# Statistics, first loads and first matmuls of a linear-attention and MLP kernel: eps as a third group, both first tiles on one queue, duplicates on GpSimd

## The chip, the cores and the metric

One core of a Trainium2 chip. The metric is the device time of one execution in microseconds (us); single executions of one kernel differ by 1 to 2 us here, so medians and ratios over several runs are given. A run is called slow when it is over 1.5% above the fastest of its kernel in the same rounds; ratios use the others, the fast runs, alone. Each profile is one execution, with its own span (a little shorter than the device time).

## The reference, cut to what matters

```python
x = A_x                                  # 1 x 2048 x 448, bf16
xn = _layernorm(x, axis=-1)              # (x - m) / sqrt(v + 1e-5)
return x + _A_ref(xn, A_wqkv, A_w_phi, A_wo) + _B_ref(xn, B_w1, B_w2)
# A: linear attention with softmax feature maps, 16 heads of 28
# B: silu(xn @ w1) @ w2, w1 is 448 x 1792
```

Everything needs xn. The kernel has sixteen tiles of 128 rows. The first tiles are normalised on VectorE, transposed on TensorE and go at once into xn @ w1 ("F1"); the later ones are prepared behind that work.

## The kernel before

The loads are issued from two queues, SP's and ScalarE's. w1 comes as three blocks of 448 KB and two small pieces:

```python
load_x(0, 1)                 # tile 0, 112 KB, SP queue
load_x(1, 2, eng="act")      # tile 1, ScalarE queue
load_w1(0, "sp")             # weight block 0 ("first")
load_w1(1, "act")            # block 1 ("second")
load_x(2, 3, eng="act")
load_w1(2, "sp")             # block 2 ("third")
# ... two last pieces of w1, tile 3; w_phi in 56-byte rows; then wqkv, wv, w2
```

The statistics of a tile, with eps added by an instruction of its own, and the power on GpSimd:

```python
bn_stats(st6[:, t, :], x_sb[:, t, :])                        # VectorE
bn_aggr(mv[:, t, :], st6[:, t, :])                           # VectorE: mean, variance
tensor_scalar(ve[:, t], mv[:, t, 1:2], EPS_LN, None, add)    # VectorE (tiles 0-3) or GpSimd
tensor_tensor(rstd[:, t], ve[:, t], neghalf, pow)            # GpSimd
tensor_scalar(xnd[:, t, a:b], x[a:b], mean, rstd, subtract, mult)   # VectorE, in parts
```

TensorE's order at the start; every TensorE instruction keeps this place:

```python
warm(10)                     # 10 pairs of 512-column matmuls on a constant
X_tr(0) ... f1a(0, 0, 0)     # transposes of tile 0; 4 pairs on block 0
X_tr(1, first part)
f1a(0, 1, 0, 1)              # pairs that alternate between block 0 and block 1
...                          # block 1, then block 2, then the last pieces of w1
X_tr(2), F1B, X_tr(3), FT_tr(0), c0(0, 0), ...
```

A "pair" is two matmuls on the two halves of the array's rows (64 rows each; the second starts at most 0.04 us after the first). So the second weight block is needed at the second pair of `f1a(0, 1, 0, 1)`.

The softmax here doesn't subtract the row's maximum and nothing guards it: scores larger than these inputs give would overflow.

## Time and profile before

| | before |
|---|---|
| device time, median of the runs beside the changed kernel | 149.38 us (148.97 to 150.09, 4 runs) |
| span of the profiled run | 147.4 us |
| TensorE busy | 142.0 us, 96% of the span |
| first matmul on w1 | 6.41 us |
| second weight block: issued, landed | 1.34 us, about 6.25 us |
| start of the long stretch without waits | 20.00 us |

How to read it: the kernel ends 127.4 us after that last moment. (The prediction starts from 149.68 us, the median of three runs.) The head ends when TensorE is through its first 20 us of work, so a change in the head shows as a shift of that one number.

### The profile page before, as it was taken

The numbers are of one execution on the slowest core, as the hardware profiler recorded it, in microseconds if no ns is written. First come the engines' busy times: TensorE is split into PE (matmuls) and PEld (weight loads), VectorE is DVE, ScalarE is ACT, GpSimd is POOL, SyncE is SP. The second block draws the span as 40 slices with busy tenths as digits, with TensorE's granted clock in tenths as the row PEclk, the third lists the DMA queues.
The fourth block names the chain that finished last, engine by engine and source line by source line (L and its number), as shares of the span: only waits on it lengthen the run. The fifth ranks groups of instructions, "written<-read, shape, count | busy, mean of one in ns | idle before, by whom it ended". The sixth has DMA issues, their size and how long they took to land.

```text
span 147.4 us, 4912 instructions
## 1 busy us (share of the span) xinstructions
PE 142.0 (96%) x2118; PEld 86.7 (59%) x2118; DVE 96.4 (65%) x182; ACT 85.3 (58%) x109; POOL 84.5 (57%) x95
## 2 busy tenths in 40 slices
PE   6999999999999999999999999999999999999990
PEld 2589965555556555555555556655566666666550
DVE  1877379999995596941077997870154874948533
ACT  4248789898758785976986758598571111011110
POOL 3326026059999959899023999999972204022220
PEclk9999999999999999999999999999999999999998
DMA  4996989965929893389730091333769234843323
GB/s 127 388 266 150 296 257 275 118 139 170 146 55 112 174 167 86 90 188 134 174 67 0 0 111 36 71 76 73 73 145 101 52 105 125 129 132 76 103 71 125
DMA packets 43710, 19.10 MB, mean 130 GB/s; under 512 B 36713, under 2 KB 43049, under 8 KB 43689
## 3 DMA queue, kind: packets, MB, share of 16 engines
q1 hardware_dynamic: 43032, 17.87, 61.6%
q10 hardware_dynamic: 656, 0.92, 1.9%
q8 instruction: 16, 0.26, 0.8%
q14 instruction: 6, 0.04, 0.1%
HBM read 8.17 MB, written 1.84 MB: 68 GB/s over the span
## 4 chain that ended last, share of the span: by engine, by line
PE 96%; DVE 0%; POOL 0%; DVEq 0%; issue 0%; ACT 0%; POOLq 0%
PE psum L448 95%; PE psum L461 1%; DVE x_sb L827 0%; DVEq L1124 0%; POOL hT L487 0%; ACT xT L466 0%; POOL neghalf L486 0%; DVEq L1113 0%; POOLq L1158 0%
## 5 line engine op out<-in xcount | busy, mean ns | idle before, releaser
L715 POOL TENSOR_TENSOR E<-E,Rk 128x896 bf16<-128x896 bf16 x32 | 53.3, 1697 | 7.1 <-DVE Rk L710 5.1
L448 PE MATMUL psum<-xT,w_sb 64*128 64x512 bf16 (+2 forms) x522 | 46.7, 323 | 0.3 <-ACT xT L466 0.2
L448 PE MATMUL psum<-w_sb,hT 64*128 64x448 bf16 x448 | 45.2, 349 | 0.0
L448 PEld LDWEIGHTS psum<-w_sb,hT 64*128 64x128 bf16 x448 | 24.1, 94 | 16.6
L708 DVE TENSOR_REDUCE Sk<-E 128x64 f32<-128x1792 bf16 x16 | 31.9, 2004 | 2.9 <-ACT E L466 2.9
L466 ACT ACTIVATE hT<-psum 128x1024 bf16<-128x1024 f32 (+1 forms) x29 | 28.0, 992 | 9.5 <-PE psum L448 9.1
L448 PEld LDWEIGHTS psum<-xT,w_sb 64*128 64x128 bf16 x522 | 25.0, 94 | 13.9 <-issue 0.3
L466 ACT ACTIVATE E<-psum 128x896 bf16<-128x896 f32 x32 | 27.4, 917 | 6.4 <-PE psum L448 5.3
L466 ACT ACTIVATE xT<-psum 128x448 f32<-128x448 f32 (+3 forms) x14 | 6.6, 475 | 32.0 <-PE psum L448 27.8
L448 PE MATMUL psum<-wqk,xT 64*128 64x448 bf16 x224 | 23.6, 349 | 0.0
L779 POOL TENSOR_TENSOR xT<-xT,x_sb 128x448 f32<-128x448 f32 x8 | 8.3, 1033 | 25.0 <-ACT xT L466 21.5
L448 PEld LDWEIGHTS psum<-wqk,xT 64*128 64x128 bf16 x224 | 12.2, 94 | 8.6
L583 POOL TENSOR_TENSOR rstd<-ve,neghalf 128x1 f32<-128x1 f32 x16 | 9.1, 569 | 7.5 <-DVE ve L581 6.8
L767 POOL TENSOR_TENSOR Ye<-Ye,x_sb 128x448 f32<-128x448 f32 x8 | 8.1, 1034 | 8.9 <-DVE Ye L765 8.9
L591 DVE TENSOR_SCALAR xnd<-x_sb,mv,rstd 128x896 bf16<-128x896 bf16 x12 | 8.3, 723 | 5.8 <-POOL rstd L583 5.7
L575 DVE BATCH_NORM_STATS2 st<-x_sb 128x6 f32<-128x448 bf16 x16 | 9.6, 604 | 3.7 <-DMA x_sb<-in_A_x_dram 3.7
L448 PE MATMUL psum<-wv_sb,xT 64*128 64x448 bf16 x112 | 12.0, 349 | 0.0
L765 DVE TENSOR_TENSOR Ye<-psum,Ye 128x448 f32<-128x448 f32 x8 | 5.0, 621 | 10.3 <-ACT Ye L466 10.2
L448 PE MATMUL psum<-wo_sb,E 64*128 64x448 bf16 x112 | 11.3, 349 | 0.0
L804 DVE TENSOR_TENSOR E<-psum,rden 128x224 bf16<-128x224 f32 x32 | 10.3, 384 | 0.4
L448 PEld LDWEIGHTS psum<-wo_sb,E 64*128 64x128 bf16 x112 | 6.2, 94 | 4.4
L448 PEld LDWEIGHTS psum<-wv_sb,xT 64*128 64x128 bf16 x112 | 5.9, 94 | 4.0
(47 smaller groups left out, 102.9 us busy)
## 6 DMA issues: line engine op xcount, KB each, us to landing
w_sb<-in_B_w_dram SPq DMA_DIRECT2D x4, 448.0 KB, 5.4
out_dram<-x_sb SPq DMA_DIRECT2D x8, 224.0 KB, 2.2
w_sb<-in_B_w_dram SPq DMA_DIRECT2D x4, 336.0 KB, 5.2
x_sb<-in_A_x_dram SPq DMA_DIRECT2D x2, 448.0 KB, 5.0
wv_sb<-in_A_wqkv_dram SPq DMA_DIRECT2D x2, 392.0 KB, 5.4
wo_sb<-in_A_wo_dram SPq DMA_DIRECT2D x14, 56.0 KB, 2.3
phT<-in_A_wqkv_dram SPq DMA_DIRECT2D x3, 224.0 KB, 4.0
w_sb<-in_B_w_dram ACTq DMA_DIRECT2D x1, 448.0 KB, 4.9
```

What stands on the lines that cost most here:

```text
L448: ins = e.matmul(dst, lhsT, rhs, start=st, stop=sp, skip_group_check=True)
L461: ins = e.transpose(dst, src, idn)
L466: return P.op("act", d_act(n), lambda e: e.activation(dst, src, func, scale=scale), reads=reads or [src], writes=writes or [dst], table=ta ...
L575: P.op("dve", 630, lambda e: e.bn_stats(st6[:, t, :], xs), [xs], [st6[:, t, :]], name="bnst", ordered=od)
L583: P.op("pool", 580, lambda e: e.tensor_tensor(rstd[:, t:t + 1], ve[:, t:t + 1], neghalf[:], ALU.pow), [ve[:, t:t + 1], neghalf[:]], [rstd[ ...
L591: dve(lambda e: e.tensor_scalar(dst, src, mv[:, t, 0:1], rstd[:, t:t + 1], ALU.subtract, ALU.mult), 734, [src, mv[:, t, 0:1], rstd[:, t:t ...
L708: dve(lambda e: e.tensor_reduce(Sk[:, t % 3, :].rearrange("p (h g) -> p h g", g=2), Er, AXL.X, ALU.add), d_dve(1792), [Er], [Sk[:, t % 3, ...
L715: pool(lambda e, Eh=Eh, Rb=Rb: e.tensor_tensor(Eh, Eh, Rb, ALU.mult), 1770, [Eh, Rh], [Eh], "phi%d" % qk)
L765: dve(lambda e: e.tensor_tensor(y, b, y, ALU.add), d_dve(D), [b, y], [y], "ye_d")
L767: pool(lambda e: e.tensor_tensor(y, y, x_sb[:, t, :], ALU.add), 1110, [y, x_sb[:, t, :]], [y], "ye_x")
L779: pool(lambda e: e.tensor_tensor(y, y, x_sb[:, t, :], ALU.add), 1110, [y, x_sb[:, t, :]], [y], "yl_x")
L804: dve(lambda e, dst=dst, src=src, rb=rb: e.tensor_tensor(dst, src, rb, ALU.mult), d_dve(224), [src, r], [dst], "o")
```

## The change

Its intent: bring xn of the first two tiles sooner and start the real work sooner. eps goes into the aggregation as a constant third group of statistics (count 0, mean 0, summed squares D*eps). Tiles 0 and 1 stand at the head of one queue, and the second weight block waits for a memset on GpSimd, so that it does not get ahead of them. Tile 0's and 1's 64-column duplicates go to GpSimd, the constant of the warm-up is written by VectorE, one warm-up pair goes, and F1 is put in another order to need the late loads later.

```diff
-        st6 = sb("st6", [128, NT, 6], F32)
+        st6 = sb("st6", [128, NT, 9], F32)
-        P.op("pool", 230, ... memset(wsrc, 1.0) ...)
+        P.op("dve", 230, ... memset(wsrc, 1.0) ...)
+        P.op("dve", 90, ... memset(st6[:, :, 6:9], 0.0) ...)
+        P.op("dve", 90, ... memset(st6[:, :, 8:9], D * EPS_LN) ...)
-        warm(10, d=427.0)
+        warm(9, d=427.0)
         load_x(0, 1)
-        load_x(1, 2, eng="act")
+        load_x(1, 2)
         load_w1(0, "sp")
-        load_w1(1, "act")
+        bd0 = P.op("pool", 300, ... memset(BD[:], 0.0) ...)
+        load_w1(1, "act", bd0)
+        load_w1(2, "sp")
         load_x(2, 3, eng="act")
-        load_w1(2, "sp")
# cut: tensor_scalar to ve goes; pow reads mv[:, t, 1:2]
# cut: xn's columns 448:512 of tiles 0 and 1 on "pool", ahead of the next tile's power
# cut: in F1, the last-64 pieces after the third block; F1B's second half ahead of X_tr(2)
-        c0(0, 0)
+        pads_init()                       # moved here, behind TensorE's mark
+        hold[0] = take()
+        for t in (2, 3):                  # 128-column pieces in place of 256
+            for u in range(2):
+                F1ph(0, hold[0], u * 256 + (t - 2) * 128, u, t * 128, 128, ...)
```

## The prediction

> **What bounds the kernel now.** I read the page's busy shares first, then the chain of waits, then the opening 13 us instruction by instruction, because everything in the diff lies there or in small statistics work off the path.

> ```profile
> PE 142.0 (96%) x2118; PEld 86.7 (59%) x2118; DVE 96.4 (65%) x182; ACT 85.3 (58%) x109; POOL 84.5 (57%) x95
> ...
> PE 96%; DVE 0%; POOL 0%; DVEq 0%; issue 0%; ACT 0%; POOLq 0%
> ```

> The first line is busy time by engine, the second the chain that ended last, by engine. TensorE is both the busiest engine and nearly the whole chain. In order of time the chain has these pieces (start us, length us, what):

> ```profile
> 0.88 0.47 POOL hT L487
> 1.35 0.05 issue
> 1.39 4.45 PE psum L448 x14
> 5.84 0.13 PE psum L461 x4
> 5.97 0.02 issue
> 5.99 0.28 ACT xT L466
> 6.28 0.14 issue
> 6.41 0.44 PE psum L448 x8
> ...
> 20.00 123.70 PE psum L448 x1725
> ```

> Three things are to be seen. From 20.00 to 143.70 there is only matmul. I summed the matmul pairs of that stretch from the program [...]: about 123 us. So this stretch runs at the array's rate, and nothing in it can be won by a helper engine. Second, the stretch from 6.41 to 20 has almost no waiting either; by the same sum it holds about 12.7 us of work in the 14.4 us from 5.63 on, and most of the missing time lies before 7.4. Third, the head: 4.45 us of warm-up matmuls on a constant, then transposes of x, an eviction, the first real matmul at 6.41. The change can only win by pulling 6.41 forward without opening holes behind it.

> What sets 6.41? The timeline of VectorE and GpSimd for the first tile:

> ```profile
> 3.19 0.63 DVE L575 BATCH_NORM_STATS2 st<-x_sb 128x6 f32<-128x448 bf16 x1 [3.19 <-DMA x_sb<-in_A_x_dram]
> 3.86 0.18 DVE L579 BATCH_NORM_AGGREGATE mv<-st 128x2 f32<-128x6 f32 x1
> 4.07 0.15 DVE L581 TENSOR_SCALAR ve<-mv 128x1 f32<-128x1 f32 x1
> 4.32 0.55 POOL L583 TENSOR_TENSOR rstd<-ve,neghalf 128x1 f32<-128x1 f32 x1 [2.25 <-DVE ve L581]
> ...
> 5.08 0.79 DVE L598 TENSOR_SCALAR xnd<-x_sb,mv,rstd 128x256 bf16<-128x256 bf16 x3
> 5.25 0.59 POOL L583 TENSOR_TENSOR rstd<-ve,neghalf 128x1 f32<-128x1 f32 x1 [0.38 <-DVE ve L581]
> 5.54 0.49 PEld L461 LDWEIGHTS psum<-ident,xnd 64*128 64x128 bf16 x10 [0.60 <-POOL rstd L583]
> ```

> x0 lands at 3.19; statistics, aggregation, the add of eps (ve), the power on GpSimd, then the first 256 columns of xn at 5.08, ready near 5.4, so its weight load is at 5.54. The warm-up queue ends at the same time: ten pairs 0.425 us apart from 1.39 make 5.64. Two limits are tied: shortening one alone wins nothing, and the change shortens both.

> [...] The ten transposes from 5.55 on average 241 ns, those after 6.35 only 190, so the clock opened near 6.2, almost 5 us after the first warm-up matmul. [...] from 4.2 us on the sum stands at some 430 GB/s, and a 448 KB weight block takes 4.0 us on SP's queue, 4.9 on ScalarE's.

> **The change part by part.**
> *eps in the aggregation.* A constant third group of statistics puts D*eps into the summed squares, so the aggregation gives var + eps. It removes ve: aggregation starts at 3.86, power at 4.32, a distance of 0.46. Without ve it is 0.18 + about 0.10 of semaphore = 0.28: power 4.14 to 4.69. VectorE also drops two ve instructions (each about 0.08 to 0.2 in its queue): second statistics near 4.0, second aggregation 4.65 to 4.83, first xn near 4.85 in place of 5.08. Gain 0.2 to 0.25. [...] For the other twelve tiles a 0.22 us GpSimd add goes (2.7 us of GpSimd in all), off the path: worth 0.
> *64-column duplicates of tiles 0 and 1 on GpSimd.* These take two instructions of about 0.30 us out of VectorE between xn0 and the evictions. On GpSimd I estimate 0.31 us: 0.22 for a one-column tensor_scalar (ve in later tiles) plus 63 x 1.48 ns, the slope between its 448- and 896-column products (1034 and 1697 ns). The first stands ahead of the second power: rstd1 runs about 5.0 to 5.6, against 5.25 to 5.84 before. So xn1 comes near 5.7 in place of 6.13: gain 0.4 for tile 1, just enough to keep up with tile 0.
> *Nine warm-up pairs.* Their start stays near 1.39 (VectorE's fill ends where GpSimd's did), their end moves from 5.64 to 1.39 + 9 x 0.425 = 5.2. Then xn is the limit: transposes near 5.3 in place of 5.63, the first real matmul near 6.05 in place of 6.41. Gain 0.35.
> *x0 and x1 on SP, second weight block behind a memset on ScalarE's queue.* x1 is issued 0.3 us later but alone behind x0, and its statistics are not due before 4.0; before it landed at 0.92 + 2.6 = 3.5. w1 block 0 landed at 1.24 + 4.0 = 5.2, over 1 us early. Block 1 landed at 6.25 (1.34 + 4.9); issued near 2.05 now, but less behind x1, I put it at 6.3 to 6.6. TensorE will ask for it at 6.3 to 6.4 (second pair of phase 1), so this may take 0 to 0.2 back. Block 2, x2 and x3 should land earlier than their 7.9, 8.1 and 9.36.
> *Order of the F1 groups, pads later.* Same number of matmul columns. Two 256-column pairs become 128-column pairs at 55 ns each against 109, so no array time is added. The third block's last-64 pieces come later, which removes the small slack of 0.35 us between their landing (8.8) and their use. The hole of about 0.05 us at 13.18 goes. The 2.5 us of pad memsets leave GpSimd's path of LN3: worth 0 to 0.1.
> *Sum.* +0.35 (start) + 0.05 (hole) + 0.05 (tile 1) - 0.1 (block 1) = 0.35. The clock takes some back: real work that starts earlier, with the warm-up starting at the same time, spends more of itself at half rate. [...] Net 0.25 to 0.3: 149.68 - 0.3 = 149.4.

> **The rivals.** (1) *The weight block takes over*: block 1, issued 0.7 us later, lands near 6.9 and TensorE waits for it at 6.3. For: it is last on the slower queue. Against: the engines carry x1 and block 0 sooner, so it shares less. It would make 149.7 to 149.9, no gain. (2) *LN3 becomes the wait*: X transposes of tiles 2 and 3 now stand back to back near 11.4 to 11.7, and before, xn3 was ready only near 12.07. For: x3 landed at 9.36 and three serial steps follow. Against: ve goes (0.2), the pads go, x3 should come 0.3 to 0.6 sooner. If it waits: 0.3 lost, 149.7. (3) *More is won than I count*: the stretch from 5.63 to 7.4 holds some 0.9 us of waiting; if the better order of VectorE closes half of it, gain 0.8, 148.9. [...]

> **Range and chances.** The change reaches at most the first 13 us of 149.68, of which about 1.7 us are not matmul work. Two per cent is 3.0 us, beyond all of it, so faster by over 2% is nearly excluded; slower by that needs a new hole of 3 us in a stretch that has none, in a program whose order on TensorE is fixed. Predicted 149.4 us. The spread of single executions (1.1 us before) exceeds the effect, so the range is 148.6 to 150.0. Chances: 0.01 faster, 0.98 within 2%, 0.01 slower.

> **What would show the steps right or wrong.** Right: no ve lines; the first power near 4.1; first xn near 4.85; transposes of x0 near 5.3; first matmul on w1 near 6.05; the chain's 123.7 us piece of the same length, beginning 0.3 us or so earlier; span near 147.1. Wrong: TensorE or its weight load idle behind a w1 landing near 6.4; a wait on xn near 11.5; the ones ending much after 1.4 on VectorE; matmuls of the first F1 group 289 ns long in place of 220 (a cold clock); the long piece longer than 124 us.

## The result, and the profile after

The changed kernel takes 153.88 us (152.52 to 154.34, 4 runs) against 149.38: slower, ratio 1.0281, 95% interval 1.0202 to 1.0359. Ratios here and below are the mean time of one kernel's fast runs over that of the other's of the same rounds, so not quite the ratio of the medians quoted beside them. The predicted 149.4, with 148.6 to 150.0 as its range, is missed.

The page of the changed kernel, busy time and the chain by engine:

```profile
PE 144.2 (95%) x2132; PEld 92.3 (61%) x2132; DVE 95.5 (63%) x179; ACT 85.4 (56%) x109; POOL 82.6 (54%) x84
...
PE 91%; DMA 5%; DVE 1%; issue 0%; POOL 0%; DVEq 0%
```

A transfer has come onto the chain. In order of time (start us, length us, what):

```profile
1.54 0.29 POOL ident L487
1.83 0.23 POOL BD L522
2.07 0.03 POOL phT L531
2.10 7.27 DMA w_sb<-in_B_w_dram
...
9.42 0.93 PE psum L447 x11
10.34 0.16 PE psum L460 x6
10.50 6.29 PE psum L447 x87
...
25.19 123.71 PE psum L447 x1716
```

The long stretch has its old length, 123.7 us, but begins at 25.19 in place of 20.00. The chain leads back through the second weight block, issued at 2.10 behind the memset of BD and landed 7.27 us later, at 9.37. The same load in the two kernels, its issues by queue (KB each, us to landing), first before, then after:

```profile
w_sb<-in_B_w_dram ACTq DMA_DIRECT2D x1, 448.0 KB, 4.9
```

```profile
w_sb<-in_B_w_dram ACTq DMA_DIRECT2D x1, 448.0 KB, 7.3
```

The start itself went as meant. VectorE's and GpSimd's timeline of the changed kernel:

```profile
2.91 0.63 DVE L577 BATCH_NORM_STATS2 st<-x_sb 128x6 f32<-128x448 bf16 x1 [1.24 <-DMA x_sb<-in_A_x_dram]
3.57 0.20 DVE L581 BATCH_NORM_AGGREGATE mv<-st 128x2 f32<-128x9 f32 x1
3.85 0.55 POOL L582 TENSOR_TENSOR rstd<-mv,neghalf 128x1 f32<-128x1 f32 x1 [1.67 <-DVE mv L581]
4.44 0.59 DVE L597 TENSOR_SCALAR xnd<-x_sb,mv,rstd 128x256 bf16<-128x256 bf16 x2
4.51 0.65 POOL L597 TENSOR_SCALAR xnd<-x_sb,mv,rstd 128x64 bf16<-128x64 bf16 x1
...
6.11 0.61 PE L447 MATMUL psum<-xT,w_sb 64*128 64x128 bf16 x8 [0.30 <-ACT xT L465]
...
6.61 0.32 PE L447 MATMUL psum<-xT,w_sb 64*128 64x128 bf16 x2
...
9.42 0.93 PE L447 MATMUL psum<-xT,w_sb 64*128 64x128 bf16 x14 [2.48 <-DMA w_sb<-in_B_w_dram]
```

ve is gone, xn stands at 4.44 in place of 5.08, and the first matmul on w1 comes 0.30 us sooner. What follows is a hole of 2.48 us, in which TensorE waits for the block, and behind it a slow stretch. The 128-column matmuls of F1, from 6.35 to 9 us before and from 9.38 to 12 us after (count, then busy us and mean ns of one):

```profile
L448 PE MATMUL psum<-xT,w_sb 64*128 64x128 bf16 x64 | 2.3, 220 | 0.2 <-ACT xT L466 0.2
```

```profile
L447 PE MATMUL psum<-xT,w_sb 64*128 64x128 bf16 x46 | 2.8, 307 | 2.5 <-DMA w_sb<-in_B_w_dram 2.5
```

307 ns in place of 220 is the half-rate clock. In this run it stays so until about 14.3 us (from there 256-column matmuls take 269 ns in place of 416, and their pairs start 109 ns apart in place of 213). The trace's clock record has its first opening at 14.28 us, and the mean granted clock of the run is 1.00 all the same: this mean leaves out the time before the first opening. In the other three runs it is 0.987 to 0.989. That fits a clock that opened and was closed again (the loads-alone trace below, 0.989), but a close shortly before the end gives nearly the same (0.990 in the run without the pieces, closed at 146.88 of 149.7 us), so it says little without a trace.

The account of the 5.19 us by which the long stretch is late: -0.30 for the earlier start; +2.48 for the hole; +2.24 for the clock, because the same 120 matmuls and transposes behind the hole took 9.42 to 16.64 here and 8.16 to 13.14 in an experiment whose clock was open (exchanged blocks, below); the remaining 0.77 is small waits, among them 0.25 us in which the weight transposes wait for an eviction of xT, and matmuls ahead of the hole at half rate.

### The profile page after: what moved, and what is told of

Same layout as the page of the kernel before. It is cut to its first block, busy times and chain, and to the rows that moved or that the text cites.

```text
span 152.5 us, 4941 instructions
## 1 busy us (share of the span) xinstructions
PE 144.2 (95%) x2132; PEld 92.3 (61%) x2132; DVE 95.5 (63%) x179; ACT 85.4 (56%) x109; POOL 82.6 (54%) x84
## 4 chain that ended last, share of the span: by engine, by line
PE 91%; DMA 5%; DVE 1%; issue 0%; POOL 0%; DVEq 0%
PE psum L447 90%; DMA w_sb<-in_B_w_dram 5%; PE psum L460 1%; DVE x_sb L826 0%; DVEq L1127 0%; DVE hT L486 0%; DVE xT L632 0%; POOL ident L487 0%; POOL BD L522 0%; DVE st L494 0%; POOL phT L531 0%
## 5 line engine op out<-in xcount | busy, mean ns | idle before, releaser
L447 PE MATMUL psum<-xT,w_sb 64*128 64x512 bf16 (+2 forms) x538 | 49.3, 333 | 2.8 <-DMA w_sb<-in_B_w_dram 2.5
L447 PEld LDWEIGHTS psum<-xT,w_sb 64*128 64x128 bf16 x538 | 27.7, 101 | 16.3 <-DMA w_sb<-in_B_w_dram 3.1
L465 ACT ACTIVATE hT<-psum 128x1024 bf16<-128x1024 f32 (+1 forms) x29 | 28.3, 995 | 11.7 <-PE psum L447 11.4
L447 PEld LDWEIGHTS psum<-w_sb,hT 64*128 64x128 bf16 x448 | 25.6, 94 | 15.2
L447 PEld LDWEIGHTS psum<-wqk,xT 64*128 64x128 bf16 x224 | 13.0, 94 | 7.8
L582 POOL TENSOR_TENSOR rstd<-mv,neghalf 128x1 f32<-128x1 f32 x16 | 8.8, 561 | 14.9 <-DVE mv L581 14.9
```

The source lines that it names most:

```text
L447: ins = e.matmul(dst, lhsT, rhs, start=st, stop=sp, skip_group_check=True)
L465: return P.op("act", d_act(n), lambda e: e.activation(dst, src, func, scale=scale), reads=reads or [src], writes=writes or [dst], table=ta ...
L582: P.op("pool", 580, lambda e: e.tensor_tensor(rstd[:, t:t + 1], mv[:, t, 1:2], neghalf[:], ALU.pow), [mv[:, t, 1:2], neghalf[:]], [rstd[:, ...
```

## The experiments

Theory A: the late second weight block makes the hole, and the hole keeps or puts the clock at half rate. Rival B: the loss comes from GpSimd's duplicates, the nine warm-up pairs or the new order of F1. All results were correct to the reference.

### The loads alone, the loads undone

The kernel before with only the new order of loads:

```diff
-        load_x(1, 2, eng="act")
+        load_x(1, 2)
         load_w1(0, "sp")
-        load_w1(1, "act")
-        load_x(2, 3, eng="act")
+        bd0 = ...memset(BD)...
+        load_w1(1, "act", bd0)
         load_w1(2, "sp")
+        load_x(2, 3, eng="act")
```

> The kernel before with only the new order of the first loads (x1 on SP behind x0, the second weight block on ScalarE's queue behind the memset of BD, the third weight block ahead of x2). Theory A (the late second weight block and the clock that stays at half rate behind the hole make the loss): the second block lands 7 us or more after its issue, TensorE waits over 1.5 us for it, 152.5 to 155 us. Rival B (the loss comes from the other parts, such as GpSimd's duplicates or the nine warm-up pairs): 149 to 150 us.

Measured: 152.81 us (152.41 to 153.91), ratio 1.0216 (1.0121 to 1.0311). The block landed at 9.12, the hole was 2.17 us. So the loads carry most of the loss by themselves (2.2% of 2.8%, with intervals that overlap); B falls for the bulk of it. Here the clock had opened before the hole and closed as it ended (open at 5.94, closed at 9.35, open again at 12.76 by the clock record), with the matmuls behind it at 301 ns:

```profile
L448 PE MATMUL psum<-xT,w_sb 64*128 64x128 bf16 x54 | 3.1, 301 | 2.2 <-DMA w_sb<-in_B_w_dram 2.2
```

The changed kernel with the loads in the old order and the memset of BD in its old place (the diff above, reversed):

> The changed kernel with the old order of the first loads. Theory A: the second block lands near 6.3 us, no wait for it of more than 0.3 us, 148.7 to 149.6 us, so level with or just ahead of the kernel before. Rival B: stays above 152 us. Rival C (nine warm-up pairs in place of ten keep the clock at half rate by themselves): no wait for weights, but the first F1 matmuls of 128 columns near 300 ns to beyond 9 us, 150 to 152 us.

Measured: 150.65 us (149.16 to 151.77), ratio 1.0026 (0.9905 to 1.0148). The block landed at 6.6, TensorE waited 0.28 us for weights, and the clock was open at 5.1 us, so rival C (nine pairs as such) isn't seen. The ratio's interval holds 1: level with the kernel before, within noise. But the median lies a microsecond above A's number, and the trace shows why: TensorE stands still in the middle of a group of matmuls, and no semaphore ends it.

```profile
17.11 0.70 PE L447 MATMUL psum<-xT,w_sb 64*128 64x256 bf16 x9
...
18.56 0.81 PE L447 MATMUL psum<-xT,w_sb 64*128 64x256 bf16 x11 [0.75 <-issue]
```

This is a second, smaller cost, of the F1 part. It is taken up below.

### What makes the block late

The changed kernel without the wait for the memset:

```diff
-        load_w1(1, "act", bd0)
+        load_w1(1, "act")
```

> The changed kernel, but the second weight block is issued on ScalarE's queue at once, without waiting for the memset of BD (at about 0.9 us in place of 2.1). If the late issue is what makes the block late: it lands by 6.2 us and the time is 149 to 149.8. If the order on SP's queue (x1 and the third weight block there) is what starves it: it still lands after 7.5 us and the time stays above 151.5.

Measured: 153.81 us (152.15 to 154.18), ratio 1.0272 (1.0169 to 1.0374). Neither branch: the block landed at 4.6 us, as early as one could wish, and the time is as bad. Now tile 1 is late, with a 448 KB block issued ahead of its 112 KB: issued at 1.25, it landed at 5.0, so after 3.75 us, where the changed kernel's took 2.28:

```profile
DVE st L577 <- DMA x_sb<-in_A_x_dram: 2.5, 2, 1.8
```

Its 1.8 us wait stands ahead of tile 0's xn in VectorE's order, so the first matmul on w1 came at 7.06. So the memset does keep the block from getting ahead of tile 1. (This run's profile also has a standstill of 1.81 us of the kind just seen. It is of the fastest of the five runs; the others, 1.3 to 2 us slower, have no trace.)

The kernel before with the late issue alone; tile 1 stays on ScalarE's queue:

```diff
+        bd0 = ...memset(BD)...
-        load_w1(1, "act")
+        load_w1(1, "act", bd0)
```

> The kernel before with one edit: the second weight block (and what follows it on ScalarE's queue) is issued behind the memset of BD, at about 2.0 us in place of 1.34; x1 stays on ScalarE's queue. If the late issue alone makes the block late: it lands past 7 us, TensorE waits for it, 151 us or more. If x1's move to SP's queue is needed too (one queue alone at work from 2.8 to 4 us): it lands by 6.8 us, the wait stays under 0.3 us, 149.5 to 150.3.

Measured: 154.24 us (153.93 to 155.24), ratio 1.0332 (1.0272 to 1.0392). The late issue is enough, and the move of tile 1 isn't needed: issued at 1.97 in place of 1.34, the block landed at 9.5. TensorE's timeline of this run and its clock by stretch (us, PEclk, DMA share, GB/s):

```profile
6.44 0.23 PE L448 MATMUL psum<-xT,w_sb 64*128 64x128 bf16 x2
9.57 0.93 PE L448 MATMUL psum<-xT,w_sb 64*128 64x128 bf16 x14 [2.91 <-DMA w_sb<-in_B_w_dram]
```

```profile
7.60:8.40 0.80, 0.74 1.04 216
8.40:9.40 1.00, 0.50 0.43 64
```

0.63 us of delay at the issue has become over 3 us at the landing. The clock record of this trace opens at 4.57, closes at 7.98, in the hole, and opens again at 14.81. Before, the third block (448 KB, on SP) went out some 0.35 us after the second; in this run it goes out 0.3 us ahead of it, and in the changed kernel within 0.1 us of it. Does it take the second's place? The changed kernel with the third block held until the first has landed:

```diff
-        load_w1(2, "sp")
+        load_w1(2, "sp", chain[0])
```

> The changed kernel, but the third weight block is issued only when the first has landed (about 5.2 us). If sharing the engines with the third block is what stretches the second: it lands by 6.7 us and the first hole falls under 0.5 us, while a new wait for the third block, landing near 8.7 to 9.3 us, may come; 150.5 to 152.5 in all. If the second block's late start and the thin stretch before it are enough: it still lands after 7 us, and the time is 152.5 to 154.5.

Measured: 153.89 us (152.64 to 154.93), ratio 1.0264 (1.0194 to 1.0334). The trace agrees with the first expectation's mechanism: the second block landed at 6.8 us in place of 9.37, and there was no wait for it. It is one trace, though, and the filler run below, whose loads are those of the changed kernel, had the block at 7.3; so holding the third is worth between 0.5 us and 2.5. The hole has moved to the third block, which landed at 10.15:

```profile
w_sb<-in_B_w_dram ACTq DMA_DIRECT2D x1, 448.0 KB, 4.7
```

```profile
10.28 3.49 PE L447 MATMUL psum<-xT,w_sb 64*128 64x256 bf16 x60 [1.57 <-DMA w_sb<-in_B_w_dram]
```

The time lies higher than the 152.5 expected at most; part of that is a standstill of 1.04 us without a semaphore, again.

Exchanging the second and third block between the queues was the miss:

```diff
-        load_w1(1, "act", bd0)
-        load_w1(2, "sp")
+        load_w1(1, "sp")
+        load_w1(2, "act", bd0)
```

> The changed kernel with the second and third weight block exchanged between the queues: the second follows the first on SP's queue, the third goes on ScalarE's behind the memset of BD. If the second block is late because it starts when the third is already ahead in the other queue and shares the engines: it lands by 7 us, the wait shrinks to under 0.7 us, but the third block comes near 9 us and may be waited for; 150.5 to 152.5. If the single queue's slow stretch from 2.8 to 4 us is all of it: the block still lands after 7.3 us and the time stays above 152.5.

Measured: 153.39 us (151.83 to 155.38, 3 of the 6 runs counted as fast, mean 152.34), ratio 1.0175 (1.014 to 1.0211). The second block, behind the first on SP, landed at 8.1 and not by 7; the third, on ScalarE's queue, at 7.3. The landing is that of the second expectation, the thin stretch, which the late-issue run contradicts (below). Two blocks in flight at once both land late here, and the one on the other queue than the first block came first. The packets of the traces show who went first: in the changed kernel the 3584-byte rows on ScalarE's queue begin only as the first block's on SP's run out (none before 4.4 us, when SP's queue had started 87). By what rule the two queues share the engines is not shown, and the trace doesn't say which engine moved which row.

```
rows of 3584 bytes started   4.0-4.4   4.4-4.8   4.8-5.2   5.2-5.6   5.6-6.0 us
before, SP / ScalarE queue   30 / 16    6 / 40    1 / 45   23 / 24   41 / 0
after,  SP / ScalarE queue   36 / 0    27 / 7    12 / 29    9 / 33   13 / 25
late issue, the same         28 / 2    32 / 4    30 / 6    17 / 20    9 / 32
```

Before, the second block was nearly through when the third began; after, it is in flight beside it to the end; with the late issue alone the third goes first (the first block has 118 of its 128 rows started by 4.0 us). The whole transfer is also thinner at first. With both tiles and the first block on one queue, the stretch from 2.8 to 4.0 us moved little; before, then after:

```profile
2.80:4.00 1.20, 1.00 1.02 302
```

```profile
2.80:4.00 1.20, 1.00 0.95 173
```

All five kernels with tile 1 on SP and the second block behind the memset (or on SP) moved 173 to 255 GB/s there, the nine others with a trace 287 to 407. But the late-issue run moved 360 there and lost most of all, so this is an addition and not the cause.

One more part is seen and not explained. A load lands in sixteen parts, and in some traces one of them comes long after the other fifteen. For the second block it was 1.2 us late in the changed kernel (fifteen by 8.2, the last at 9.37), 1.7 with the loads alone and 0.9 with the late issue, but also 1.0 with the loads undone and 1.1 in the run with eps only, further down. In those traces the loads behind it straggle too; in the other nine the gap of the second block is under 0.2 us (the held-third trace has 0.65 on the third block). So it comes with the old order of loads as well as with the new one, and makes up a good part of the holes above: without it the loads-alone hole would be about 0.5 us (an estimate: 2.17 less 1.7). Whether the unprofiled runs had it, nothing here tells.

### The clock

The changed kernel with seven more warm-up pairs where TensorE waits:

```diff
         X_ev(1, 3, WA)
+        warm(7, d=427.0)
         f1a(0, 1, 0, 1)
```

> The changed kernel with seven more warm-up pairs of 512 columns put on TensorE where it waits for the second weight block (about 3.0 us of work at half rate). Theory A with the clock as the second half of the loss: the clock opens 3 us or so earlier, F1 behind the hole runs at 216 to 220 ns in place of 300 to 310, and 1 to 2.5 us come back: 151.5 to 153. If the clock has no part in it: no gain, 153.5 to 154.5.

Measured: 152.03 us (151.34 to 153.72), ratio 1.0137 (1.0032 to 1.0242). As expected of a part of the clock: F1 behind the fill ran at 217 ns, the clock record opens at 5.03, before the fill, and stays open, and the granted clock of the fast runs was 0.998 to 1.0 (0.987 to 0.989 in three of the changed kernel's four). The block landed at 7.3 in this profile, so the two parts aren't cleanly divided by it; TensorE's timeline:

```profile
6.37 1.69 PE L447 MATMUL psum<-hT 64*128 64x512 bf16 x14
7.89 0.61 PE L447 MATMUL psum<-xT,w_sb 64*128 64x128 bf16 x16
```

With useless matmuls in the hole the kernel is about 1.9 us faster by the medians, 2 by the ratios; the two were measured in different rounds, and their intervals overlap. How much of that is an earlier landing, and how much the clock, these runs don't tell apart.

### The rest of the change

The statistics part alone: the kernel before with eps, ones on VectorE, nine warm-up pairs and the duplicates on GpSimd.

> The kernel before with the statistics part of the change alone: eps as a third group, ones on VectorE, nine warm-up pairs, the 64-column duplicates of tiles 0 and 1 on GpSimd; loads, order of F1, 256-column pieces and pad memsets as before. If the idle stretch of 0.75 to 1.8 us in the runs before it (always at TensorE's 345th matmul, no semaphore) and 0.3 to 0.4 us around the second transposes come from the new order of F1: both are gone, 148.8 to 149.6 us, ratio 0.993 to 1.000. If they come from the statistics part: it stays at 150 to 151.5.

Measured: 149.57 us (148.71 to 151.44), ratio 0.9982 (0.9953 to 1.001). No standstill over 0.3 us: the first branch holds. xn comes 0.5 us sooner (4.57) and the first matmul on w1 0.6 us sooner (5.82), but little of it reaches the end, because TensorE now meets the weights: three waits for w1, 0.7 us in all, where before had none. In this trace the head is bound by the loads as soon as the statistics are faster.

The same with the duplicates on VectorE, as before:

```diff
-        P.op("pool" if a == D and t < 2 else "dve", ...)
+        P.op("dve", ...)
```

> As the run with the statistics part alone, but the 64-column duplicates stay on VectorE. GpSimd took 0.65 us for one of them where 0.31 was estimated, and the second tile's power waits behind it. If that eats the gain of the second tile: its xn comes 0.3 us sooner here, and the time is 148.6 to 149.4, ratio 0.99 to 0.998, at or below the other run. If the duplicates on GpSimd were worth it: 149.2 to 150.

Measured: 150.6 us (149.19 to 153.58), ratio 1.003 (1.0 to 1.0061), so not faster but rather slower than the other: a miss. The mechanism is there, as VectorE's xn of tile 1 shows, with the duplicates on GpSimd and then on VectorE:

```profile
5.93 0.35 DVE L596 TENSOR_SCALAR xnd<-x_sb,mv,rstd 128x256 bf16<-128x256 bf16 x1 [0.36 <-POOL rstd L581]
```

```profile
5.59 0.34 DVE L596 TENSOR_SCALAR xnd<-x_sb,mv,rstd 128x256 bf16<-128x256 bf16 x1
```

Tile 1 gains 0.34 us and TensorE waits for the first weight block anyway (first matmul on w1 at 6.18 there, 0.45 us of it waiting for the load). That load straggles: fifteen of its parts had landed by 5.0 us, the last at 6.13, so this one profile can't show what the duplicates are worth. The two profiled spans are equal, 147.6 and 147.7; what makes the rest of the runs 0.5% slower stays open.

Undoing the 128-column pieces as well as the loads:

```diff
-        hold[0] = take()
-        # four groups of 128-column pairs
+        c0(0, 0)
```

> The changed kernel with the old loads (as in the run of that name) and also with the two 256-column pairs of the first group put back in place of the 128-column pieces. If TensorE runs dry at a fixed place in its instruction stream: the idle stretch moves 32 instructions, so 16 matmuls, later in the program, to the transposes of the second half of the weights, or is hidden there, and 0 to 0.8 us are won against the 150.65 of that run. If a transfer or a buffer is behind it, the stretch stays at the same matmul of the program (the tenth of the group of twenty).

Measured: 150.25 us (149.06 to 153.1), ratio 1.0031 (1.0006 to 1.0056). The 0.4 us against the run with the loads undone were measured in other rounds and are within noise. The standstill has moved later in the program, into the transposes of the second half of the weights, as the first branch said (this profile is of a slow run, so only the place is read from it):

```profile
18.34 0.25 PE L460 MATMUL psum<-ident,phT 64*128 64x64 bf16 x5
19.37 0.49 PE L460 MATMUL psum<-ident,phT 64*128 64x64 bf16 x17 [0.79 <-issue]
```

And the 128-column pieces alone, put into the kernel before:

> The kernel before with only the two 256-column pairs of the second half cut into 128-column pieces: the same array time, 16 more matmuls and 16 more weight loads. [...] an idle stretch of 0.3 to 1.8 us with no semaphore at TensorE's 345th matmul, 149.9 to 151. [...] no stretch, 149.4 to 149.9, ratio 0.998 to 1.002.

Measured: 150.93 us (149.33 to 154.09), ratio 1.0047 (1.0016 to 1.0078). The array's time is nearly the same (pairs of 128 columns start 55 to 56 ns apart, those of 256 columns 109, in the trace of the kernel before), and the standstill is there:

```profile
18.10 0.93 PE L448 MATMUL psum<-xT,w_sb 64*128 64x256 bf16 x13 [0.67 <-issue]
```

Counting TensorE's matmuls in the traces, the standstill follows the 345th in all seven that have one (loads undone, no wait for the memset, filler, exchanged blocks, held third block, no pieces, pieces alone), at whatever line and time that is. In each a 16 KB packet of the instruction queue had started 2.4 to 2.8 us before TensorE went on (3.6 us in the pieces-alone run). The stops last 0.67 to 1.81 us. A semaphore or a buffer does not explain the fixed count; that TensorE's own instructions come late, with such a packet, would. In the kernel before, the packet starts at 14.5 and the 346th matmul runs at 18.1, without a stop; with the pieces TensorE is there at 17.2 and waits until 18.1. That the packet is what TensorE waits for is inference from the place and the times: no record shows it. The run without the pieces has a standstill too, so they are enough for one, not needed for it.

The kernel before once more:

> The kernel before, unchanged, for a second trace of it: 149 to 150.2 us, second weight block landed by 6.5 us, no hole of TensorE over 0.3 us before the 123.7 us piece, and the clock open by 7 us.

Measured: 148.91 us. Second block landed at 5.9, no hole, clock open at 5.5, and the long stretch began at 19.79, so the first trace was no exception.

## Why the prediction was wrong

**The step that failed** is the term of the sum for "block 1": "issued near 2.05 now, but less behind x1, I put it at 6.3 to 6.6 [...] so this may take 0 to 0.2 back". It was issued at 2.10 and landed at 9.37; the hole was 2.48 us. The working counted what stood ahead of the block (x1 gone) and not what would now overtake it or run beside it: the third block on SP. That the late issue is enough is shown: 0.63 us become over 3, with the third block's rows in front. How the nearly 3 us beyond the forecast divide in the changed kernel is not: the block landed at 6.8 with the third held, at 7.3 with the third beside it (filler), and at 9.37 where its last part straggled by 1.2.

**Rival 1** named the right wait with the wrong size: landing "near 6.9", and "149.7 to 149.9" for the time. It also stopped at the hole.

**The clock** was priced as a small average, an estimate that took the sum of 0.35 to a net of 0.25 to 0.3. It is neither small nor apart from the hole: in the two traces with a hole of 2.2 or 2.9 us an open clock closed, and in the changed kernel's own the clock, not yet open ahead of the hole, stayed at half rate for 4.9 us behind it. Hole and clock together are 4.7 of the 5.19 us. The sign named for a shut clock, 289 ns in place of 220 (an estimate), came: 291 ns for the last pair ahead of the hole, 307 behind it. Four traces opened as early as 4.31 to 4.62. (The trace of the kernel before opened at 6.54, not near 6.2.)

**"slower by that needs a new hole of 3 us in a stretch that has none"** was the argument for 0.98 within 2%. A stretch without waits was taken for a stretch with slack. The second block had 0.6 us of it: landed at 6.25, and the group of sixteen matmuls that needs it began at 6.80. The change asks 0.2 us earlier (6.61) and lands 3.1 us later.

**"Same number of matmul columns [...] no array time is added"** is right about the array and incomplete: the pieces alone cost 0.5%, with a standstill of 0.67 us in their trace.

**What was right.** Aggregation to power took 0.28 us, as worked out (3.57 to 3.85). Transposes of x0 at 5.33 against 5.3, the first matmul on w1 at 6.11 against 6.05; but here luck helped. xn was said to be the limit, at 4.85 with the warm-up done by 5.2. xn came at 4.44, in part because x0 had landed 0.28 us earlier than before, and the transposes waited for the warm-up, which began at 1.52 in place of 1.39. (The third group cost the aggregation 0.02 us, 0.20 against 0.18.) That VectorE's fill with ones would end where GpSimd's did was the estimate: it took 0.48 against 0.52 us, but started later, at 0.98. The long stretch kept its length, and the sum of about 123 us for it holds by the starts of the pairs in the trace of the kernel before: 189 ns apart for 448 columns (447 pairs), 216 for 512 (147 pairs), 25 to 29 for the shorter ones (268 pairs). Rival 2's wait on xn did not come (the transposes of tiles 2 and 3 ran at 16.64 without one).

**Also wrong.** The third block, x2 and x3 were said to land earlier; they landed at 9.5, 9.9 and 10.5, later than the 7.9, 8.1 and 9.4 of before.

**The duplicate on GpSimd** took 0.65 us where 0.31 was estimated, and where VectorE's took a mean of 0.31 in the kernel before. What made it so long, no run isolates. Beside it the parts of xn took at most 0.36 us in the changed kernel and 0.34 before, and the powers 0.55 and 0.56 against 0.55 and 0.59. The duplicate's effect, 0.34 us on tile 1, lay hidden behind the loads.

**What stays open:** the straggling sixteenth part of a load, and how much of the late landing is its own; the 0.5% between the two statistics runs; how the clock's and the hole's shares divide in the unprofiled runs. By the measure of 2% only the changed kernel and the late issue are slower outright; the intervals of the other versions with a late block reach below it. No version here beats the kernel before beyond doubt; the statistics part alone comes nearest, at 0.9982 with an interval that includes 1.

## What to carry to other kernels

Before moving a load, list for every load the time it lands and the time it is first needed, and ask which other load will be in flight beside it in the new order; a delay at the issue can put a load beside or behind the next big one (0.63 us here became over 3 at the landing). Before putting a landing down to the order, look at its sixteen parts, and at a second trace. A hole of TensorE in the head is paid twice if the clock is shut behind it (2.48 and 2.24 us in the changed kernel). Work cut into smaller instructions of the same total length was not free here (0.5%, with a standstill of 0.67 us in the trace); that the instruction stream is the cause is inferred.
